# Output projection by quarters of the columns in a two-layer memory transformer with linear attention, with displaced rows through a DRAM scratch and a new order of work

## Chip, cores and metric

The kernel runs on one core of a Trainium2 chip. The metric is the device time of one execution in microseconds (us); the time of a kernel is the median over several runs. A profiled execution gives a trace of every instruction and every DMA packet of that one core.

## What is computed

The input is 2048 rows of 512 numbers. Four blocks follow each other, each adding to its input x: a recurrent-memory attention (A), a linear attention (B), A again and B again, with the same weights.

```python
# A, on h = layernorm(x); 64 segments of 32 rows, 32 heads of 128, 8 memory rows
mem = mem0
for s in range(64):
    h = concat([mem, xs[s]])                    # 40 x 512
    q, k, v = h @ Wq, h @ Wk, h @ Wv            # 40 x (32 heads x 128)
    p = softmax(mask(q @ k.T * 128 ** -0.5))    # per head, 40 x 40; memory rows see all
    o = (p @ v) @ Wo                            # 40 x 512
    mem = o[:8]; out[s] = o[8:]                 # mem feeds the next segment
x = x + out
# B, on layernorm(x): 32 heads of 16, phi(t) = where(t > 0, t + 1, exp(t)) + 1e-6
x = x + (phi(q) @ (phi(k).T @ v) / (phi(q) @ sum(phi(k)) + 1e-6)) @ wo
```

The memory rows make the 64 segments of a layer A one chain: segment s+1 can't project its memory rows before the output projection of segment s.

## The kernel before, in words

**Order of the work.** Every operation is recorded by `add` (L1632) as a node with a key such as (layer, step, 'out', 3). The table `PLACE` (L16 to L1555) gives each node a rank and, for copies that ScalarE (ACT) or VectorE (DVE) can both do, the engine. `schedule` (L1681) sorts all nodes by rank, gives PSUM banks, and `emit` (L1788) writes each engine's instructions in that order. So each engine runs a fixed list, in order, and waits on semaphores where a node needs another engine's result. Work that hangs on nothing late (the linear attention, the projections of rows that are known early) is put between the links of the chain by rank alone.

**Tiles on TensorE (PE).** Nearly all matmuls use a quarter of the array's columns: four matmuls with 32 columns of weights each, at tile positions (0, 0), (0, 32), (0, 64), (0, 96), write the four groups of 32 partitions of a PSUM bank. Such a four is the unit below. Each matmul stands in the program with a weight load of its own (LDWEIGHTS), except where the weights stay (`again`, L2075, seen in the trace as L2077).

**One segment step.** A block of 32 columns of hT holds 8 memory rows and 24 rows of the segment; the last 8 rows of each of four segments are collected in one more block, the left rows of the group (G counts groups of four segments, 128 rows). A step does:

- `kq0`, `kq1`, `v` (`project`, L2171, matmuls L2191 and L2077): keys, queries and values of the block, 512 columns a matmul; copies and 32x32 transposes turn them (L1954, L1955, L2210).
- `mem0`, `mem1` (`mem_attention`, L2295): scores (L2317, L2325), exp (L2332, L2336), values of the memory rows (L2353), division and transposes (L2358, L2360) into oTb.
- `out` (`out_proj`, L2431): the output projection of the memory rows of this segment and the other rows of the segment before it. Its operand is 32 rows by 4096 (32 heads by 128), and Wo_sb is 4096 by 512. The four of a tile position j splits as j = 2k + d: k picks one half of the contraction and d one half of the columns. So 16 fours of 256 columns (L2446) leave two partial sums for each half of the columns, one in partitions 0 to 63 and one in 64 to 127. A copy of the whole tile to outW_sb in float32 (128x256, L1954) is followed by a DVE addition of the two halves (64x256, L2458) into y_sb.
- `next` (`next_mem`, L2467): eight float32 matmuls (L2476) with outW_sb as weights and the selection matrix selm_sb as the moving operand add the two halves of the memory rows, transpose them, and a 32-column copy puts them into hT of the next segment.
- `x` (`x_attention`, L2373): the other rows' part of the attention (L2384, L2396, L2403, L2368, L2406, L2416, L2423, L2428).
- `res` (`residual`, L2495): `rows_out` (L2484) moves the 24 rows of y_sb straight to dx_sb in two DMAs, one issued by GpSimd (POOL) and one by SyncE (SP), both through `x_move` (L1970); in the last step of a group the left rows are projected by another `out_proj` and moved in eight small DMAs, and DVE adds dx_sb to x_sb (L2525). The layernorm of B and its sums (`b_in`, L2671) follow.

There are 162 output projections: 65 urgent ones and 16 of left rows in each of two layers. In the last group of a layer there is no move for the final rows; `pick` (L2506) adds them on PE from y_sb.

## Time and profile before

| what | value |
|---|---|
| median of 3 runs | 1513.69 us (1512.41 to 1515.43) |
| the profiled execution | 1513.92 us |
| its span, first to last instruction | 1512.0 us |
| granted TensorE clock | 0.998 |
| PE busy | 1458.4 us |
| DVE busy | 1227.5 us |
| ACT busy | 934.3 us |
| POOL busy | 199.5 us |
| DMA | 81639 packets, 60.26 MB |

How to read it: busy time of an engine is the union of its instructions' times. A matmul's recorded time includes its way through the array (a 128x256 one is recorded with 273 ns, though the fours follow each other faster), so a busy PE is not a PE at its peak; the pace is read from the starts of rows that follow each other in the timeline. PEld is the weight loading of PE, which runs beside the matmuls. "issue" as a releaser is idle time of an engine for which the profile shows nothing that it waited for. Queue q8 is the DMA queue that brings instructions. The kernel fills one core, so only that core's trace exists.

### The profile page before, as it was taken

How to read it: one execution, taken by the hardware profiler on the slowest of the kernel's cores; microseconds unless marked ns; L12 is line 12 of the kernel's file. 1: busy time of each engine (PE TensorE's matmuls, PEld its weight loads, DVE VectorE, ACT ScalarE, POOL GpSimd, SP SyncE). 2: the span in 40 equal slices, each digit the busy share in tenths (PEclk: the TensorE clock that was granted, in tenths of full speed). 3: DMA queues.
4: the chain of work that ended last, by engine and by line, in shares of the span. 5: the costliest groups of instructions: out<-in, count | busy, mean ns of one | idle time of the engine just before them, and what ended most of it. 6: DMA issues, size and time to landing. Idle time of an engine off the chain costs nothing.

```text
span 1512.0 us, 90803 instructions
## 1 busy us (share of the span) xinstructions
PE 1458.4 (96%) x43597; PEld 835.8 (55%) x39357; DVE 1227.5 (81%) x4035; ACT 934.3 (62%) x2686; POOL 199.5 (13%) x398
## 2 busy tenths in 40 slices
PE   7999999999999999999999999999999999999998
PEld 3455555555565555555545555555555555555554
DVE  4788888888888788788878888788887888887777
ACT  2566556665665656565566767666666755666656
POOL 3011110111111011111111110111111011111010
PEclk9999999999999999999999999999999999999999
DMA  9310100100000010001310101011110111011034
GB/s 390 106 35 21 35 14 23 25 24 24 25 21 11 23 25 24 25 23 32 64 25 21 28 18 27 25 28 28 25 22 20 26 24 28 20 28 32 16 49 134
DMA packets 81639, 60.26 MB, mean 40 GB/s; under 512 B 64040, under 2 KB 74600, under 8 KB 79720
## 3 DMA queue, kind: packets, MB, share of 16 engines
q1 hardware_dynamic: 67944, 37.58, 9.7%
q0 software_dynamic: 13152, 16.75, 4.0%
q8 instruction: 324, 5.31, 1.5%
q14 instruction: 59, 0.48, 0.1%
q10 hardware_dynamic: 160, 0.14, 0.0%
HBM read 25.57 MB, written 11.67 MB: 25 GB/s over the span
## 4 chain that ended last, share of the span: by engine, by line
PE 81%; DVE 8%; DMA 5%; ACT 3%; issue 1%; SPq 1%; POOL 0%; DVEq 0%
PE pb L2191 36%; PE pb L2446 18%; PE pb L2077 13%; PE pb L2089 3%; PE pb L2396 2%; PE pb L2633 2%; DMA dx_sb<-y_sb 2%; PE pb L2353 2%; PE pb L2416 2%; ACT arena_sb L1954 2%; PE pb L2317 1%; PE pb L2476 1%; DVE arena_sb L2210 1%; DVE arena_sb L1955 1%; DMA Wk_sb<-in_A_Wk_dram 1%
## 5 line engine op out<-in xcount | busy, mean ns | idle before, releaser
L1954 ACT ACTIVATE arena_sb<-pb 128x512 bf16<-128x512 f32 (+3 forms) x1021 | 512.0, 529 | 285.7 <-PE pb L2077 125.5
L2191 PE MATMUL pb<-Wk_sb,arena_sb 128*32 128x512 bf16 x4192 | 363.5, 382 | 5.5 <-DVE arena_sb L1955 2.5
L2191 PE MATMUL pb<-Wv_sb,arena_sb 128*32 128x512 bf16 x4608 | 340.1, 379 | 1.2 <-ACT arena_sb L1954 0.9
L2446 PE MATMUL pb<-Wo_sb,arena_sb 128*32 128x256 bf16 x10368 | 328.2, 273 | 5.7 <-issue 1.3
L2210 DVE STREAM_TRANSPOSE arena_sb<-arena_sb 128x256 f32<-128x256 f32 x640 | 259.9, 426 | 43.0 <-ACT arena_sb L1954 37.6
L2446 PEld LDWEIGHTS pb<-Wo_sb,arena_sb 128*32 128x32 bf16 x10368 | 261.5, 97 | 43.5 <-DVE arena_sb L2360 16.7
L2191 PE MATMUL pb<-Wq_sb,arena_sb 128*32 128x512 bf16 x3088 | 257.5, 379 | 1.3 <-DVE arena_sb L1955 1.1
L1971 POOL DMA_DIRECT2D dx_sb<-y_sb x246 | 125.0, 512 | 921.6 <-DVE y_sb L2458 401.3
L2191 PEld LDWEIGHTS pb<-Wk_sb,arena_sb 128*32 128x32 bf16 x4192 | 118.7, 97 | 184.9 <-issue 95.4
L2368 ACT ACTIVATE arena_sb<-pb,arena_sb 128x128 bf16<-128x128 f32 x536 | 166.8, 368 | 71.3 <-DVE arena_sb L2403 27.6
L2077 PE MATMUL pb<-Wq_sb,arena_sb 128*32 128x512 bf16 x2032 | 203.1, 381 | 0.0
L2191 PEld LDWEIGHTS pb<-Wv_sb,arena_sb 128*32 128x32 bf16 x4608 | 120.9, 96 | 94.5 <-issue 13.0
L2370 DVE TENSOR_TENSOR arena_sb<-pb,arena_sb 128x384 bf16<-128x384 f32 (+2 forms) x366 | 153.8, 421 | 7.9
L1955 DVE CAST arena_sb<-pb 128x512 bf16<-128x512 f32 (+2 forms) x239 | 117.8, 495 | 48.3 <-PE pb L2077 33.2
L1954 ACT ACTIVATE outW_sb<-pb 128x256 f32<-128x256 f32 (+1 forms) x156 | 59.7, 383 | 140.9 <-PE pb L2446 112.9
L2191 PEld LDWEIGHTS pb<-Wq_sb,arena_sb 128*32 128x32 bf16 x3088 | 86.1, 97 | 84.8 <-issue 24.2
L2384 DVE TENSOR_TENSOR arena_sb<-arena_sb,wx_sb 128x640 bf16<-128x640 bf16 x256 | 117.9, 472 | 2.9 <-ACT arena_sb L2336 2.1
L2396 PE MATMUL pb<-arena_sb 128*32 128x130 bf16 x3072 | 105.9, 220 | 1.4 <-issue 1.2
L2406 DVE STREAM_TRANSPOSE arena_sb<-arena_sb 128x192 f32<-128x192 f32 x256 | 93.2, 364 | 15.2 <-ACT arena_sb L2368 13.3
L2458 DVE TENSOR_TENSOR y_sb<-pb,outW_sb 64x256 bf16<-64x256 f32 x162 | 68.7, 424 | 38.2 <-ACT outW_sb L1954 34.4
L2077 PE MATMUL pb<-Wk_sb,arena_sb 128*32 128x512 bf16 x928 | 91.8, 379 | 0.1
L2396 PEld LDWEIGHTS pb<-arena_sb 128*32 128x32 bf16 x3072 | 68.4, 96 | 30.7 <-issue 7.8
(128 smaller groups left out, 1808.5 us busy)
## 6 DMA issues: line engine op xcount, KB each, us to landing
Wk_sb<-in_A_Wk_dram SPq DMA_DIRECT2D x1, 4096.0 KB, 14.9
Wq_sb<-in_A_Wq_dram SPq DMA_DIRECT2D x1, 4096.0 KB, 24.2
Wv_sb<-in_A_Wv_dram SPq DMA_DIRECT2D x1, 4096.0 KB, 33.6
Wo_sb<-in_A_Wo_dram SPq DMA_DIRECT2D x8, 512.0 KB, 23.2
xs_scratch<-x_sb POOLq DMA_DIRECT2D x32, 128.0 KB, 2.2
pq_scratch<-arena_sb POOLq DMA_DIRECT2D x27, 128.0 KB, 2.3
x_sb<-xs_scratch POOLq DMA_DIRECT2D x16, 128.0 KB, 3.4
dx_sb<-y_sb SPq DMA_DIRECT2D x126, 12.0 KB
```

The source lines that it names most:

```text
L1954: return e.activation(o() if callable(o) else o, i() if callable(i) else i, ACTF.Copy)
L1955: return e.tensor_copy(o() if callable(o) else o, i() if callable(i) else i)
L1971: add(eng, lambda e: e.dma_start(o, i), 0.55 if eng == "pool" else 0.66, reads=reads, writes=writes, dsem="%s%d" % (kind, k), lat=lat + (0 ...
L2077: return pe.add_instruction(mybir.InstMatmult(name=nc.get_next_instruction_name(), engine=mybir.EngineType.PE, ins=[pe.lower_ap(x), pe.low ...
L2191: r = pe.matmul(o, blk[:, c, :], w, start=(c == 0), stop=(c == 3), tile_position=(0, 32 * j))
L2210: add("dve", lambda v: v.transpose(dst, src(img[:, k, :].bitcast(F32))), 0.445, reads=[("img", k, h) for h in range(2)], writes=[dkey])
L2368: x = e.activation(o[:, u, :], i()[:, u, :], ACTF.Copy, scale=r[:, u:u + 1])
L2370: return e.tensor_tensor(o, i(), r.unsqueeze(2).to_broadcast([128, n, 128]), ALU.mult)
L2384: add("dve", lambda v, b=b: v.tensor_tensor(Px[:, b, :].rearrange("p (n j x) -> p n j x", n=20, j=4), PQ[:, r2, b, 64:224].rearrange("p (n ...
L2396: r = pe.matmul(pv.f32()[32 * i:32 * i + 32, 130 * k:130 * k + 130], cols(b, k, i), vimg[:, r2, 4 * b + i, :], start=True, stop=True, skip ...
L2406: add("dve", lambda v, b=b, k0=k0: v.transpose(oTb[:, s1, b, :, :, k0:k0 + 3].rearrange("p h j k q e -> p k (h j) (q e)").bitcast(F32), ox ...
L2446: r = pe.matmul(tl.f32()[32 * j:32 * j + 32, 0:256], oT[:, b, f, n, :, :, e], Wo_sb[:, 16 * b + 4 * n + 2 * f + e, 256 * d:256 * d + 256], ...
```

## The change

`out_proj` takes the four of a tile position as four quarters of the columns, each over the whole contraction: 32 fours of 128 columns instead of 16 of 256, and no partial sums. The result, 32 rows by 4 quarters in 128 partitions, goes into y_sb by one 128-column copy (ACT or DVE); outW_sb and the addition are gone. `next_mem` has four bfloat16 matmuls of 32 columns with y_sb as weights. y_sb has three buffers: two that take turns for the segments and one for left rows.

A row of y_sb now lies in four partitions, so displaced rows go through DRAM: each segment's 128x128 tile is written to `dy_scratch` by one POOL DMA (runs of 256 bytes), the left rows by four DMAs (two POOL, two SP), and one SP DMA per group reads 128 rows of 512 back into dx_sb; in the last group of a layer three DMAs do. `pick` has 16 matmuls of 128 columns instead of 8 of 256. The memset of half of y_sb is gone; two small tiles move within the arena.

All of `PLACE` is new: every rank, and in many places the choice between ACT and DVE.

```diff
-        def out_proj(oT, keys, urgent, end=False):
...
-                        for j in range(4):
-                            k, d = divmod(j, 2)
-                            n, f, e = 2 * k + (u + i) // 4, (u + i) // 2 % 2, (u + i) % 2
-                            r = pe.matmul(tl.f32()[32 * j:32 * j + 32, 0:256], oT[:, b, f, n, :, :, e],
-                                          Wo_sb[:, 16 * b + 4 * n + 2 * f + e, 256 * d:256 * d + 256], start=(hh == 0 and i == 0),
-                                          stop=(hh == 7 and i == 1), tile_position=(0, 32 * j))
+        def out_proj(oT, keys, k):
...
+                        for h in range(2):
+                            n, f, e = 2 * h + (u + i) // 4, (u + i) // 2 % 2, (u + i) % 2
+                            for j in range(4):
+                                r = pe.matmul(tl.f32()[32 * j:32 * j + 32, 0:128], oT[:, b, f, n, :, :, e],
+                                              Wo_sb[:, 16 * b + 4 * n + 2 * f + e, 128 * j:128 * j + 128],
+                                              start=(hh == 0 and i == 0 and h == 0), stop=(hh == 7 and i == 1 and h == 1),
+                                              tile_position=(0, 32 * j))
...
-            nd = evac(outW[cc, v, :], lambda: tl.f32()[cc, 0:256], 256, tiles=[tl], writes=[("outW", w)])
...
-            add("dve", lambda e: e.tensor_tensor(y, tl.f32()[a, 0:256], outW[c, v, :], ALU.add),
-                c_dve(256), reads=[("outW", w), "y0"], tiles=[tl], writes=[yk], quad=(2, 0) if urgent else (2, 1))
+            evac(y_sb[:, k, :], lambda: tl.f32()[:, 0:128], 128, tiles=[tl], writes=[("y", k)])
...
         def next_mem(s):
...
-            for h in range(2):
-                def mm(pe, h=h):
-                    for j in range(4):
-                        o = 128 * h + 32 * j
-                        r = pe.matmul(tl.f32()[32 * j:32 * j + 32, 16 * h:16 * h + 16], outW[:, w, o:o + 32],
-                                      selm_sb[:, :], start=True, stop=True, tile_position=(0, 32 * j))
+            def mm(pe):
+                for j in range(4):
+                    r = pe.matmul(tl.f32()[32 * j:32 * j + 32, 0:32], y_sb[:, k, 32 * j:32 * j + 32], selm_sb[:, :],
+                                  start=True, stop=True, tile_position=(0, 32 * j))
...
-        def rows_out(k, G, moves):
...
-                    x_move(dx_sb[dst:dst + n, G % 2, 256 * d:256 * d + 256], y_sb[32 * d + src:32 * d + src + n, k, :], k,
-                           [("y", k)], [("dx", G % 2, dst, d)], ("dy", "dz")[d], ("pool", "sp")[d])
+        def dy_view(G):
+            return dy_dram[layer * NT + G].rearrange("(g r) (q x) -> q g r x", g=4, q=4)
...
+            for q in range(4):
+                x_move(dy_view(G)[q, :, 32:40, :], y_sb[32 * q:32 * q + 32, k, :], q, [("y", k)], [("dyl", layer, G, q)], "dz",
+                       ("pool", "sp")[q % 2])
...
+            x_move(dy_view(G)[:, g, 0:32, :], y_sb[:, w, :], w, [("y", w)], [("dy", layer, G, g)], "dy")
...
+                    x_move(dx_sb[:, G % 2, :], dy_dram[layer * NT + G].rearrange("(g r) x -> g r x", g=4)[:, 8:40, :], G % 2,
+                           [("dy", layer, G, i) for i in range(4)] + [("dyl", layer, G, q) for q in range(4)], [("dx", G % 2)], "ddx", "sp")
```

## The prediction

> **What bounds the kernel now.** I read the page first: busy time by engine, then the shares of the chain that ended last.

> ```profile
> span 1512.0 us, 90803 instructions
> PE 1458.4 (96%) x43597; PEld 835.8 (55%) x39357; DVE 1227.5 (81%) x4035; ACT 934.3 (62%) x2686; POOL 199.5 (13%) x398
> PE 81%; DVE 8%; DMA 5%; ACT 3%; issue 1%; SPq 1%; POOL 0%; DVEq 0%
> q8 instruction: 324, 5.31, 1.5%
> ```

> PE is the limit: it idles 53.6 us (1512.0 - 1458.4), and 81% of the chain is PE's own work. What PE's time is made of is read from the starts of rows in the timeline of PE; columns are start, duration, line, form, count.

> ```profile
> 701.89 1.93 PE L2446 MATMUL pb<-Wo_sb,arena_sb 128*32 128x256 bf16 x64
> 703.64 0.82 PE L2633 MATMUL pb<-arena_sb 128*32 128x512 bf16 x12
> 704.30 0.32 PE L2476 MATMUL pb<-selm_sb,outW_sb 128*32 128x16 f32 x16
> 704.45 0.24 PE L2396 MATMUL pb<-arena_sb 128*32 128x130 bf16 x4
> ...
> 705.00 0.40 PE L2191 MATMUL pb<-Wk_sb,arena_sb 128*32 128x512 bf16 x4
> 705.22 0.40 PE L2077 MATMUL pb<-Wq_sb,arena_sb 128*32 128x512 bf16 x4
> ...
> 711.11 0.27 PE L2704 MATMUL pb<-arena_sb 128*32 128x32 bf16 x16
> 711.21 0.29 PE L2416 MATMUL pb<-arena_sb 128*32 128x130 bf16 x8
> ...
> 1483.77 0.62 PE L2089 MATMUL pb<-arena_sb 128*32 128x128 bf16 x32
> 1484.21 0.60 PE L2633 MATMUL pb<-arena_sb 128*32 128x512 bf16 x8
> ```

> From start to next start: a projection's 64 matmuls take 1.75 us (109 ns a four); the float32 group of `next` 0.15 us; a four of 512 columns 0.22 us; a four of 32 columns 25 ns; a four of 128 columns 55 ns (0.44 us for 8).

> The second limit is easy to miss. Queue q8 brought 324 packets. PE and PEld together ran 43597 + 39357 = 82954 instructions, and 82954 / 324 = 256: each packet is a page of 256 PE instructions. How fast can pages come? The waits of PE put down to "issue" (line, total us, times, longest), one of them in the timeline, and the windows around it (bounds, length, then busy us and instructions of PE and PEld) answer:

> ```profile
> PE pb L2476 <- issue: 4.5, 3, 1.6
> PE pb L2446 <- issue: 1.3, 4, 0.4
> PE pb L2396 <- issue: 1.2, 3, 0.7
> PE pb L2416 <- issue: 0.6, 1, 0.6
> ```

> ```profile
> 627.55 0.24 PE L2476 MATMUL pb<-selm_sb,outW_sb 128*32 128x16 f32 x2
> 629.42 0.28 PE L2476 MATMUL pb<-selm_sb,outW_sb 128*32 128x16 f32 x11 [1.63 <-issue]
> ```

> ```profile
> 618.60:626.90 8.30, 7.34 (x211) 5.02 (x199) 6.78 (x24) 6.23 (x20) 1.64 (x3) 1.00 0.25 68
> 627.00:629.40 2.40, 0.79 (x46) 0.59 (x35) 0.99 (x3) 0.95 (x3) 0.52 (x1) 1.00 0.04 10
> 629.40:630.60 1.20, 1.18 (x35) 0.69 (x30) 0.78 (x6) 0.05 (x1) 0.00 (x0) 1.00 0.14 34
> 1163.41:1165.97 2.56, 2.56 (x132) 2.23 (x132) 2.41 (x12) 1.87 (x7) 0.00 (x0) 1.00 0.26 51
> ```

> The DMA view of these windows has no q8 row for 618.6 to 626.9 and none for 629.4 to 630.5, and one packet each here (627.0 to 629.5, then 629.4 to 630.6):

> ```profile
> q8 instruction: 1, 0.02, 2.2%
> ```

> ```profile
> q8 instruction: 1, 0.02, 5.8%
> ```

> So for 8.3 us no page arrived, PE ran some 410 instructions and then stood still inside `next` until 2.4 us after the late packet began; the next page was asked for 1.1 us after that. With no page in reserve a page costs **2.4 + 1.1 = 3.5 us**, or 73 instructions per us. PE's mean demand is 82954 / 1512 = 55 per us, so today this shows only as 7.6 us of issue waits. The last window shows how much a dense stretch may run ahead: 264 instructions in 2.56 us without a wait, 0.94 us less than 3.5.

> **The change part by part.**

> *Matmuls of the projection.* 16 fours of 256 columns become 32 of 128: 32 x 55 ns = 1.76 us against 1.75. With 57 ns a four (a little over the row) it is +0.07. I take +0.03 us, times 162 projections: **+5 us** (0 to +11).

> *`next`.* 0.15 us becomes one four of 32 columns, 0.025: -0.12 us x 126 = **-15 us**, all on PE (the count is in the row below, 2016 / 16). `pick` keeps its pace (16 x 128 columns for 8 x 256). Setup copies: nothing, they stand beside the weights' loading.

> ```profile
> L2476 PE MATMUL pb<-selm_sb,outW_sb 128*32 128x16 f32 x2016 | 40.2, 186 | 6.4 <-issue 4.5 <-ACT outW_sb L1954 1.2 <-DVE outW_sb L1955 0.2
> L2458 DVE TENSOR_TENSOR y_sb<-pb,outW_sb 64x256 bf16<-64x256 f32 x162 | 68.7, 424 | 38.2 <-ACT outW_sb L1954 34.4
> L1954 ACT ACTIVATE outW_sb<-pb 128x256 f32<-128x256 f32 x124 | 47.6, 384 | 129.7 <-PE pb L2446 102.8 <-PE pb L2396 24.9 <-PE pb L2711 1.4
> ```

> *Copies.* DVE loses 162 additions, 68.7 us; the copies, 0.384 us now, halve their columns. Neither engine is the limit, so this is worth only PE's waits on them: at most the 46 us of idle time left without issue. The addition stands behind the chain, the copy in it; the new order has both engines carrying other copies in the room gained. I take **-20 us** (-46 to +20, since an entirely new order can also place a link too tightly).

> *Displaced rows.* Per segment one POOL DMA replaces one of POOL and one of SP; per group four replace eight, and an SP load is added that waits for all of them. Queued behind that load on SP are the transposes of layernorm, behind the addition on DVE everything of the chain.

> ```profile
> xs_scratch<-x_sb POOLq DMA_DIRECT2D x32, 128.0 KB, 2.2
> x_sb<-xs_scratch POOLq DMA_DIRECT2D x16, 128.0 KB, 3.4
> L2525 DVE TENSOR_TENSOR x_sb<-x_sb,dx_sb 128x512 bf16<-128x512 bf16 x30 | 12.2, 406 | 5.8 <-DMA dx_sb<-y_sb 4.9 <-issue 0.8
> ```

> Nearest rows: a write to DRAM lands in 2.2 us, a load in 3.4. The built order of the changed kernel has about 3.3 us of PE work between write and load and 3.7 between load and addition in most groups, so both legs are covered: **0 us** (-5, today's waits there gone, to +30, one us late in each of 30 groups).

> *Instructions.* This is the largest term. 162 projections get 64 more matmuls and 64 more loads each (+20736), `next` sheds 3024: 100666, or 393 pages. A projection is now 256 instructions in 1.76 us: a full page in half of what a page costs. With the 192 instructions of a segment's attention (scores, values: 14 fours at 56 ns, 10 at 25 to 30) a step has a dense run of some 448 instructions in 2.8 us, 160 per us against 73, and after it projections of 512 columns with some 25 to 37 per us, during which only one page can be fetched ahead. A page wholly inside the dense run leaves PE dry for 3.5 - 1.76 = 1.7 us, less what it had in hand (0.94 by the last window): 0.8 to 1.7 us, in most of 128 steps.

> For the sum I cut the order of the changed program (it holds no times) into pages of 256 and gave each page its PE time by the paces above. Of 393 pages 212 last under 3.5 us, short by 223 us together: the upper end, nothing in hand. Against 2.56 us 133 pages are short by 55 us: the lower end, the full 0.94 in hand at every page. The same ledger of the kernel before gives 41 and 0.5 us, and 7.9 us against 3.0, where the trace shows 7.6. Against 2.8 and 3.0 the changed order gives 91 and 124 us. I take their middle, 108, less the 8 paid already: **+100 us** (+50 to +215).

> [...]

> *Sum*, against the profiled execution's own span: 1512 + 5 - 15 - 20 + 0 + 100 = 1582. Outside the span lie 1.9 us (1513.92 - 1512.0): **1584 us**. That execution stands 0.2 us above the median of 1513.69, which changes nothing here.

> **The rivals.**

> 1. *Pages keep up* (the faster side). If pages are asked for further ahead than the stall suggests, or twice at a time, only the PE work and the waits remain: 1512 + 5 - 15 - 15 + 2 = 1489. For it: only 11 issue waits among 324 pages, and the window of 264 instructions in 2.56 us. Against it: the measured 2.4 + 1.1 us. It decides from a page cost of about 1.9 us downwards, where a projection's page no longer waits. Chance 0.13.

> 2. *The weight load sets the pace.* One of 97 ns for each four instead of 55 would make a projection 32 x 0.101 = 3.2 us:

> ```profile
> L2446 PEld LDWEIGHTS pb<-Wo_sb,arena_sb 128*32 128x32 bf16 x10368 | 261.5, 97 | 43.5 <-DVE arena_sb L2360 16.7
> ```

> 261.5 us over 2592 fours are 101 ns a four, which fits loads one after another as well as four beside each other. Price (3.23 - 1.75) x 162 = +240: 1512 - 15 + 240 - 10 + 2 = 1729. Against it: the 32 matmuls at 1483.77, each with its own load, took 0.44 us. Chance 0.02. [...]

> 3. *The detour is late.* Both DRAM legs one us over the placed distance in 30 groups, with DVE held in order: 60 us on top of rival 1, 1549. The 2.2 and 3.4 us rows speak against it. Chance 0.02.

> 4. *Nothing moves*: PE's savings are eaten by new waits, 1511 to 1517. PE's share of 96% speaks against exact balance. Chance 0.04.

> **How the numbers follow.** Forecast 0.79, at 1584. Its range: the page term from 55 (less 8) with all waits gone, 1512 - 10 - 46 + 47 + 2 = 1505, up to 150 with no wait gained, 1512 - 10 + 150 + 2 = 1654; the 215 needs nothing ever in hand, which the 2.56 us window excludes. I give 1500 to 1655, which leaves rivals 1 and 2 and the tails outside. A difference of 0.2% is about what a measurement of this kernel can tell from no change. Slower by more: forecast and rivals 2 and 3, 0.83. Within: 0.03. Faster: rival 1 and the edge of rival 4, 0.14.

> **What would show it.** q8 near 393 packets. PE waits put down to issue near 100 us instead of 7.6, of 0.5 to 1.7 us, inside or right after the projection's matmuls, about one per segment, with a q8 packet begun some 2.4 us before each end. Where PE is not dry, a projection of 128 matmuls in 1.75 to 1.8 us. the addition into x_sb waiting under 10 us for its load. DVE near 1170 us busy. Wrong if: issue waits stay under 20 us (rival 1), the projection runs evenly at 100 ns a four (rival 2), or DVE waits for dx_sb by 50 us (rival 3).

## The result, and the profile after

The changed kernel takes **1662.82 us** (median of four runs, 1658.15 to 1667.08), the kernel before beside it 1514.56 (1512.41 to 1515.71): a ratio of 1.098 (95% interval 1.0944 to 1.1016), 148 us more. The forecast was 1584 in a range of 1500 to 1655: the direction and the mechanism hold, the size does not.

The page of the changed kernel: span, busy time by engine, the chain that ended last by engine, and the queue that brings instructions.

```profile
span 1656.3 us, 108079 instructions
PE 1486.8 (90%) x52469; PEld 872.7 (53%) x48229; DVE 1198.1 (72%) x3943; ACT 874.2 (53%) x2518; POOL 201.7 (12%) x338
PE 86%; issue 8%; DVE 3%; DMA 1%; ACT 1%; SPq 0%
q8 instruction: 394, 6.46, 1.6%
```

PE idles 169.5 us where it idled 53.6. "issue" has 8% of the chain for 1%, DVE 3% for 8% and DMA 1% for 5%. The queue brought 394 pages of 256 PE instructions for 324. The waits of PE in the same run (line, what ended the wait, total us, times, longest us):

```profile
PE pb L2433 <- issue: 72.1, 80, 2.0
PE pb L2387 <- issue: 20.7, 19, 1.8
PE pb L2182 <- issue: 12.9, 17, 2.4
PE pb L2407 <- issue: 9.3, 8, 2.0
PE pb L2455 <- issue: 5.1, 5, 1.9
PE pb L2455 <- ACT y_sb L1953: 3.9, 15, 0.4
```

L2433 is the projection, L2387 and L2407 the values of the segment's attention, L2455 `next`. All issue waits together, with four smaller lines, are 128.3 us for 7.6. How one of them looks is read in the timeline of PE (start, duration, line, form, count, idle time before it):

```profile
705.56 0.62 PE L2433 MATMUL pb<-Wo_sb,arena_sb 128*32 128x128 bf16 x32
706.01 0.20 PE L2316 MATMUL pb<-arena_sb 128*32 128x64 bf16 x4
...
706.14 0.84 PE L2433 MATMUL pb<-Wo_sb,arena_sb 128*32 128x128 bf16 x48
706.81 0.21 PE L2316 MATMUL pb<-arena_sb 128*32 128x64 bf16 x4
...
708.48 0.35 PE L2433 MATMUL pb<-Wo_sb,arena_sb 128*32 128x128 bf16 x11
709.64 0.27 PE L2433 MATMUL pb<-Wo_sb,arena_sb 128*32 128x128 bf16 x5 [0.82 <-issue]
...
710.91 1.45 PE L2433 MATMUL pb<-Wo_sb,arena_sb 128*32 128x128 bf16 x87
713.39 0.55 PE L2433 MATMUL pb<-Wo_sb,arena_sb 128*32 128x128 bf16 x25 [1.03 <-issue]
```

Where PE is not dry, 32 matmuls take 0.45 us and 48 take 0.67: 56 ns a four, so the projection itself is not slow. But it stops inside a four that has begun, after 11 and after 87 matmuls, where no semaphore stands. From 709.64 to 713.39, a page apart, are 3.75 us. The DMA views of 707.0 to 709.6 and of 710.6 to 713.3 show one packet of queue q8 each; the row of the first view is:

```profile
q8 instruction: 1, 0.02, 2.7%
```

By the trace's packet starts these begin at 707.29 and 710.79, so PE resumes 2.4 and 2.6 us after its packet begins.

The two parts of the change that could have been late are in the groups by line: the addition of the displaced rows into x (count, busy us, mean ns, idle time before it) and the copy of the projection on ACT.

```profile
L2516 DVE TENSOR_TENSOR x_sb<-x_sb,dx_sb 128x512 bf16<-128x512 bf16 (+1 forms) x32 | 12.9, 403 | 0.3 <-DMA dx_sb<-dy_scratch 0.3
L1953 ACT ACTIVATE y_sb<-pb 128x128 bf16<-128x128 f32 x137 | 37.9, 277 | 198.5 <-PE pb L2433 155.3 <-PE pb L2387 41.1 <-PE pb L2701 1.7
```

The detour through DRAM costs 0.3 us of waiting in the whole run.

To give the page term one number I cut each run's PE and PEld instructions, in the order of their starts, at every 256th, and added up by how much the matmul at each cut starts later than the pace of its shape would have it. The kernel before has 19.6 us at its cuts, the changed one 162.8: **+143 us** of the 144.3 by which the spans differ. At all other places the late starts are 71.9 and 70.2 us.

The waits themselves show where the cuts are. Counting in the instructions of PE's sequencer that the trace also holds (some 164, nearly all of them waits on semaphores), all 141 issue waits of the changed kernel and all 11 of the kernel before come 193 or 194 instructions beyond a multiple of 256: each stands at the edge of a page.

How much is put down to the cuts depends a little on the count. A second one takes the pace of each shape from the medians of the same two traces and counts lateness wherever PE falls behind that pace. It gives 17 and 169 us at the cuts (+152), 88 and 86 elsewhere (-2) and 5 us less work at full pace, together the 144.

### The profile page after: what moved, and what is told of

Read it like the earlier page. It is cut to its first block, busy times and chain, and to the rows that moved or that the text cites. A ratio compares the mean times of both kernels' runs of the same rounds, so it can differ in the third digit from the quotient of the medians.

```text
span 1656.3 us, 108079 instructions
## 1 busy us (share of the span) xinstructions
PE 1486.8 (90%) x52469; PEld 872.7 (53%) x48229; DVE 1198.1 (72%) x3943; ACT 874.2 (53%) x2518; POOL 201.7 (12%) x338
## 4 chain that ended last, share of the span: by engine, by line
PE 86%; issue 8%; DVE 3%; DMA 1%; ACT 1%; SPq 0%
PE pb L2182 39%; PE pb L2433 19%; PE pb L2070 14%; PE pb L2387 3%; PE pb L2082 3%; PE pb L2623 2%; PE pb L2344 2%; PE pb L2407 2%; PE pb L2308 2%; DMA Wk_sb<-in_A_Wk_dram 1%; PE pb L2455 1%; DVE arena_sb L1954 1%; PE pb L2316 1%; ACT arena_sb L1953 0%; ACT y_sb L1953 0%
## 5 line engine op out<-in xcount | busy, mean ns | idle before, releaser
L2433 PE MATMUL pb<-Wo_sb,arena_sb 128*32 128x128 bf16 x20736 | 369.8, 220 | 74.3 <-issue 72.1
L2182 PE MATMUL pb<-Wk_sb,arena_sb 128*32 128x512 bf16 x4192 | 376.6, 385 | 16.9 <-issue 7.1
L2433 PEld LDWEIGHTS pb<-Wo_sb,arena_sb 128*32 128x32 bf16 x20736 | 321.0, 97 | 133.6 <-issue 90.3
L2182 PE MATMUL pb<-Wq_sb,arena_sb 128*32 128x512 bf16 x3088 | 266.6, 380 | 4.6 <-issue 2.7
L1954 DVE CAST arena_sb<-pb 128x512 bf16<-128x512 f32 (+2 forms) x277 | 134.1, 487 | 156.2 <-PE pb L2387 50.6
L1971 POOL DMA_DIRECT2D dy_scratch<-y_sb x186 | 124.8, 672 | 1002.6 <-ACT y_sb L1953 528.8
L2070 PE MATMUL pb<-Wq_sb,arena_sb 128*32 128x512 bf16 x2032 | 211.5, 385 | 1.6 <-issue 1.6
L2361 DVE TENSOR_TENSOR arena_sb<-pb,arena_sb 128x384 bf16<-128x384 f32 (+2 forms) x402 | 176.7, 441 | 9.6
L2359 ACT ACTIVATE arena_sb<-pb,arena_sb 128x128 bf16<-128x128 f32 x403 | 128.2, 368 | 94.7 <-DVE arena_sb L2414 35.8
L1953 ACT ACTIVATE y_sb<-pb 128x128 bf16<-128x128 f32 x137 | 37.9, 277 | 198.5 <-PE pb L2433 155.3
L2387 PE MATMUL pb<-arena_sb 128*32 128x130 bf16 x3072 | 118.7, 221 | 20.7 <-issue 20.7
L2387 PEld LDWEIGHTS pb<-arena_sb 128*32 128x32 bf16 x3072 | 71.9, 96 | 49.3 <-issue 33.3
L2070 PE MATMUL pb<-Wk_sb,arena_sb 128*32 128x512 bf16 x928 | 93.0, 379 | 0.6 <-issue 0.6
L2407 PE MATMUL pb<-arena_sb 128*32 128x130 bf16 x2048 | 71.1, 221 | 10.5 <-issue 9.3
## 6 DMA issues: line engine op xcount, KB each, us to landing
xs_scratch<-x_sb POOLq DMA_DIRECT2D x32, 128.0 KB, 2.5
dx_sb<-dy_scratch SPq DMA_DIRECT2D x30, 128.0 KB
pq_scratch<-arena_sb POOLq DMA_DIRECT2D x27, 128.0 KB, 2.3
```

The costliest lines, as they stand in the source:

```text
L1953: return e.activation(o() if callable(o) else o, i() if callable(i) else i, ACTF.Copy)
L1954: return e.tensor_copy(o() if callable(o) else o, i() if callable(i) else i)
L1971: add(eng, lambda e: e.dma_start(o, i), 0.55 if eng == "pool" else 0.66, reads=reads, writes=writes, dsem="%s%d" % (kind, k), lat=lat + (0 ...
L2070: return pe.add_instruction(mybir.InstMatmult(name=nc.get_next_instruction_name(), engine=mybir.EngineType.PE, ins=[pe.lower_ap(x), pe.low ...
L2182: r = pe.matmul(o, blk[:, c, :], w, start=(c == 0), stop=(c == 3), tile_position=(0, 32 * j))
L2359: x = e.activation(o[:, u, :], i()[:, u, :], ACTF.Copy, scale=r[:, u:u + 1])
```

## The experiments

My theory: the changed kernel is slower because a dense run of PE instructions uses pages up faster than one page at a time can be fetched. Its rivals: each four's weight load sets the pace, the detour or the new order is late, or pages keep up. All times below are medians beside runs of the kernel before on the same chip; runs 4 and 5, which measure PE alone, are single executions.

**1. The kernel before, with twice the projection's instructions.** Order, detour and sum of halves stay as they were.

```diff
-    for j in range(4):
-        ... tl[.., 0:256] <- Wo_sb[.., 256 * d:256 * d + 256]
+    for c in range(2):
+        for j in range(4):
+            ... tl[.., 128 * c:128 * c + 128] <- Wo_sb[.., 256 * d + 128 * c:256 * d + 128 * c + 128]
```

> The kernel before, with one edit: each 256-column matmul of the output projection becomes two of 128 columns, each with its own weight load (256 instructions a projection instead of 128). Order of work, sum of halves, copies, DMAs all stay. Theory (pages of 256 PE instructions cost some 3.5 us each): 103,853 instructions, 405 pages; short by 270 us against 3.5 us a page, where the changed kernel's were short by 223 and lost 143 more than before, so some 150 to 175 us are added: 1665 to 1690 us. Rival 'the new order of work is to blame': 1515 to 1525. Rival 'the DRAM detour or its DMAs are to blame': 1515 to 1525. Rival 'weight loads set the pace of narrow matmuls': slower too, with even 100 ns fours and few issue waits.

1721.35 us beside 1509.98, ratio 1.1406 (1.1363 to 1.1448): +211 us, 31 us above the range that I expected. The page and the largest wait of PE:

```profile
q8 instruction: 405, 6.64, 1.6%
```

```profile
PE pb L2448 <- issue: 96.6, 90, 2.5
```

With no detour, no new order and the same columns computed, instructions alone cost more than the whole change. 217 us are late at the page cuts, 198 more than before.

**2. The same split, but the second half of each pair keeps the weights.** As many loads as before, 10368 more matmuls.

```diff
+    if c:
+        r = again(pe, y, oT[..], x, s, t, (0, 32 * j), True)
```

> The kernel before with each 256-column matmul of the output projection split into two of 128 columns, the second four reusing the weights that are loaded (192 instructions a projection: 128 matmuls, 64 loads). Pages theory: 93,485 instructions, 365 pages, short by 139 us against 3.5 us a page (before: 41), so some 50 to 75 us are added: 1565 to 1590 us. Rival 'weight loads set the pace': no more loads than before, so 1515 to 1525. Rivals order and detour: 1515 to 1525.

1588.34 us, ratio 1.0513 (1.0483 to 1.0543): +78 us, 365 pages, 93 us late at the cuts. This is the upper edge of what the pages theory gave, and no weight load was added. The projection now stands on two lines: the first half of each pair on L2453, the second on L2077, together with other matmuls that keep their weights. The largest waits of PE, and the projection's own group on L2077 (count, busy us, mean ns, idle time before it):

```profile
PE pb L2453 <- issue: 15.4, 20, 1.6
PE pb L2077 <- issue: 11.6, 18, 1.2
PE pb L2396 <- issue: 11.3, 14, 1.6
```

```profile
L2077 PE MATMUL pb<-Wo_sb,arena_sb 128*32 128x128 bf16 x10368 | 328.3, 219 | 11.4 <-issue 11.0
```

So the projection has 15.4 + 11.0 = 26.4 of the 65.4 us of issue waits in this run, 40%; it has 72.1 of 128.3 in the changed kernel and 96.6 of 178.5 in run 1, more than half. The rest falls on the work beside it: the stall goes to whoever stands at the page's end.

**3. The changed kernel with the wide matmuls of before.** The order, the copies and the detour stay changed.

```diff
-    for h in range(2):
-        for j in range(4):
-            ... tl[.., 0:128] <- Wo_sb[.., 128 * j:128 * j + 128]
+    for j in range(4):
+        ... tl[.., 0:256] <- Wo_sb[.., 256 * d:256 * d + 256]
```

> The changed kernel with its new order, copies, next and DRAM detour, but the projection's matmuls are those of before: 16 fours of 256 columns (128 instructions). Left out: the two halves of the contraction are not added, and only 128 of the 256 columns are copied on. Pages theory: 80,124 instructions, 312 pages, short by 20 us against 3.5 us (before: 41), so nearly all of the loss goes: 1490 to 1510 us. Rivals 'new order' and 'DRAM detour': 1640 to 1665, as the changed kernel. Weight loads: 1490 to 1510 too.

1489.26 us, ratio 0.9871 (0.9848 to 0.9895). The page and the projection's issue waits:

```profile
PE 1440.2 (97%) x42101; PEld 799.7 (54%) x37861; DVE 1194.7 (81%) x3943; ACT 874.0 (59%) x2518; POOL 201.5 (14%) x338
q8 instruction: 313, 5.13, 1.4%
```

```profile
PE pb L2433 <- issue: 0.9, 2, 0.7
```

With 81 pages fewer the late starts at the cuts are 7.9 us, and everything else of the change is no longer slow. The order and the detour are not the cause. But this run leaves out the sum of the halves, and that turned out to matter (runs 7 to 10).

**4. What a page costs, PE alone.** Bursts of fours, one kind after another, with slow stretches (kept weights, 512 columns) between them; the last burst beside loads of 4 MB from DRAM.

```diff
+    sparse(pe)
+    fours(pe, 512, 128, True)
+    sparse(pe)
+    fours(pe, 512, 128, False)
+    sparse(pe)
+    fours(pe, 256, 256, True)
+    sparse(pe)
+    fours(pe, 1024, 32, True)
+    sparse(pe).then_inc(s_pe, 1)
+    fours(pe, 512, 128, True)
```

> A measurement of the page cost by itself. Nothing of the reference is computed: the output is zeros, and PE runs five dense stretches on a matrix of ones, with a stretch of 90 fours of 512 columns without loads before each, so that pages can be brought ahead. Stretches: 512 fours of 128 columns with loads (4096 instructions, 16 pages); the same without loads (2048, 8 pages); 256 fours of 256 columns with loads (2048, 8 pages); 1024 fours of 32 columns with loads (8192, 32 pages); the first again beside 4 MB loads from DRAM. Pages theory: 16 x 3.5 = 56 us, about 28, about 28, 32 x 3.5 = 112, and the last longer than the first if other DMAs slow the page; PE runs at full pace for at most 512 instructions before it first stands still. [...]

The kernel took 401.53 us. In the timeline of PE the count is one of matmuls; where each has a load, 128 of them are a page:

```profile
24.18 2.51 PE L32 MATMUL pb<-one_sb 128*32 128x128 bf16 x167
27.98 1.97 PE L32 MATMUL pb<-one_sb 128*32 128x128 bf16 x128 [1.30 <-issue]
31.44 1.97 PE L32 MATMUL pb<-one_sb 128*32 128x128 bf16 x128 [1.49 <-issue]
...
79.08 1.66 PE L32 MATMUL pb<-one_sb 128*32 128x128 bf16 x93 [1.76 <-issue]
...
148.19 28.36 PE L32 MATMUL pb<-one_sb 128*32 128x256 bf16 x1028
...
200.06 1.19 PE L32 MATMUL pb<-one_sb 128*32 128x32 bf16 x128 [2.00 <-issue]
...
307.73 0.62 PE L32 MATMUL pb<-one_sb 128*32 128x32 bf16 x5 [2.52 <-issue]
...
335.03 3.56 PE L32 MATMUL pb<-one_sb 128*32 128x128 bf16 x128 [2.98 <-issue]
...
368.74 3.18 PE L32 MATMUL pb<-one_sb 128*32 128x128 bf16 x128 [2.88 <-issue]
```

The dense burst runs 167 matmuls and their loads at full pace, 334 instructions, then exactly one page between stalls: (79.08 - 27.98) / 14 = **3.65 us a page**. By the count of 256 the burst began some 80 instructions before the end of a page, so the 334 are that rest and one whole page more. With 32 columns, where a page holds a quarter of the columns, it is (307.73 - 200.06) / 30 = 3.59, at a clock granted at only 0.51: the price belongs to the instructions, neither to the width of the matmul nor to the clock. At 256 columns with loads (1028 matmuls without a break; the next row starts at 176.36) a page lasts 3.5 us and nothing stalls. Beside the loads from DRAM six pages take 33.7 us, 5.6 each. By the trace's packet starts 3.1 to 4.2 us pass there between PE's restart and the next packet after four of five restarts, where 1.1 do after the loads. The clock was granted at 0.74 there, and a page's 128 matmuls are recorded with up to 3.61 us for 1.97, but that is not the whole reason: one of these pages ran at full clock, PE ran out of instructions at 347.25, and the next packet began 1.6 us after that; in the first burst it begins 0.8 to 0.9 us before PE runs out.

These rows also settle the weight loads: the first 167 matmuls carry one each and run at 55 ns a four.

**5. How much is in hand when a dense run begins.** PE alone again, in cycles of 784 instructions, so that the page cut moves by 16 each time; the dense run has 256, 448 and 640 of them.

```diff
+    for dense, slow in ((32, 66), (56, 42), (80, 18)):
+        for i in range(16):
+            fours(pe, dense, 128, True)
+            r = fours(pe, slow, 512, True)
```

> No part of the kernel's computation: PE alone runs 16 cycles each of a dense run (fours of 128 columns, each matmul with its load) and a slow run (fours of 512 columns with loads): 256 + 528, 448 + 336 and 640 + 144 instructions, 784 a cycle, so that the page boundary moves by 16 instructions each cycle. It asks what PE has in hand when a dense run of the changed kernel's length begins. [...]

The waits and parts of the timeline (676.46 us in all):

```profile
PE pb L31 <- issue: 52.3, 46, 2.0
```

```profile
24.25 259.54 PE L31 MATMUL pb<-one_sb 128*32 128x128 bf16 x6439
284.79 12.26 PE L31 MATMUL pb<-one_sb 128*32 128x128 bf16 x384 [1.00 <-issue]
...
482.97 12.26 PE L31 MATMUL pb<-one_sb 128*32 128x128 bf16 x384 [1.05 <-issue]
496.55 1.97 PE L31 MATMUL pb<-one_sb 128*32 128x128 bf16 x128 [1.32 <-issue]
500.30 6.64 PE L31 MATMUL pb<-one_sb 128*32 128x128 bf16 x256 [1.77 <-issue]
...
669.90 4.32 PE L31 MATMUL pb<-one_sb 128*32 128x128 bf16 x89 [1.50 <-issue]
```

The 16 cycles with 256 dense instructions run without a stall (6272 of the first row's 6439 matmuls; the other 167 begin the next kind). With 448 there is one stall a cycle, in 14 of 16 cycles, 13.2 us from 284.79 to 482.97. With 640 the other 32 waits add 39.1 us. Each stall also costs about 0.2 us that counts as busy (128 matmuls at 55 ns a four are 1.76, the rows above say 1.97). So a cycle loses (13.2 + 14 x 0.2) / 16 = 1.0 us and (39.1 + 32 x 0.2) / 16 = 2.8 us. Against them stands an estimate for the same time in hand at every page: the instructions of a cycle cut into pages, 55 ns a dense four and 0.22 us a slow one, each page counted as far as it is short of a threshold. With 2.56 us (0.94 in hand) a cycle of 448 loses 0.7 us and one of 640 1.3, with the 2.9 that I took 1.1 and 2.0, with 3.5 to 3.6 (nothing in hand) 1.9 to 2.0 and 3.2 to 3.4. The measured 1.0 lies between the first two, the 2.8 between the last two. No one number fits both. What fits both: **something is in hand once for each dense run, not at every page**. Cut at the pages, page and stall last 3.1 us here after a page that did not stall, and 3.6 after one that did.

**6. The kernel before, with the copied halves in bfloat16**, the part of the change that takes the float32 passes out of `next`.

```diff
-    selm_sb = sb("selm_sb", [128, 16], F32)
+    selm_sb = sb("selm_sb", [128, 16])
-    outW = sb("outW_sb", [128, NW - 1, 256], F32)
+    outW = sb("outW_sb", [128, NW - 1, 256])
```

> The kernel before, its order untouched, with one thing changed: the copied half sums and the 16-column selection matrix are bfloat16 instead of float32, so that `next` is 8 bfloat16 matmuls in place of 16 float32 passes (each half sum is rounded to bfloat16 before the halves are added). Pages: 324 become about 316. If the float32 form of `next` is all that PE's own work can gain from the new projection (step `next`), PE loses 0.10 us x 126 = 13 us and the time falls to 1495 to 1502. If that time only turns into waits on the copies ahead of it, it stays within 3 us of the kernel before.

1505.29 us beside 1510.91, ratio 0.9965 (0.995 to 0.9981). That is 5.6 us less, between the two expectations, and the only kernel here that computes all and beats both. PE's busy time falls by 10.4 us, from 1458.4, so the work saved reaches the time only in part:

```profile
PE 1448.0 (97%) x42589; PEld 810.7 (54%) x38349; DVE 1226.1 (82%) x4035; ACT 933.7 (62%) x2686; POOL 199.7 (13%) x398
```

**7 to 10. The changed order with wide matmuls, and the halves really added.** Run 3 left the sum out. Run 7 sends both halves through the scratch and adds both into x; run 8 brings each half back by one load instead of two; run 9 adds the halves on DVE right behind the copy, so that the scratch carries no more than in the changed kernel; run 10 places that addition up to four places later.

Run 7, against run 3:

```diff
+    evac(y_sb[:, k, :], lambda: tl.f32()[:, 0:256], 256, ..)
+    dy_dram = [2 * NT, 4, 160, 256]
+    for h in range(2):
+        add("dve", .. x[0:n, :] + dx_sb[0:n, 2 if h else G % 2, :])
```

> The changed kernel's order of work, bfloat16 copies and route through DRAM scratch, but with the 256-column projection of before (halves of the contraction, 64 matmuls): the halves are copied once in bfloat16, each goes to the scratch by itself, and both are loaded and added into x (two additions a group), `next` has 8 matmuls. Pages about 316. Pages theory: everything that cost the changed kernel its time is gone, and what it won stays: 1488 to 1500, issue waits of PE under 10 us. Rival (the sum of the halves, which the run with wide matmuls in the changed order left out, is what the change bought its gain with): 1508 or more, with PE or DVE waiting for the second addition or its loads.

Run 8, against run 7:

```diff
-    dy_dram = [2 * NT, 4, 160, 256]
+    dy_dram = [2 * NT, 160, 4, 256]
```

> The kernel of the run with both halves sent through the scratch, with one thing changed: the scratch keeps the four quarters of a row side by side, so that each group's two halves come back by one load each (two DMAs on SP's queue in place of four, same bytes). In the run before it the additions into x waited 43.9 us for these loads (39 waits, 1.1 us each), and four loads took SP 2.21 us to issue, 0.55 each. If the detour was late by SP's issuing, the last load starts 1.1 us earlier and most of that wait goes: under 15 us of waits on dx_sb and 1495 to 1525. If the order itself is worse with halves, or the doubled bytes are what is late, the wait stays at 30 us or more and the time at 1540 or more.

Run 9, against run 3:

```diff
+    evac(yp_sb[:, k, :], lambda: tl.f32()[:, 0:256], 256, ..)
+    add("dve", .. y_sb[0:64, k, :] = tl.f32()[64:128, 0:256] + yp_sb[0:64, k, :])
```

> The changed kernel's order and its route through DRAM scratch, with the 256-column projection of before, whole: the halves are copied in bfloat16, `next` takes the halves (8 matmuls), and one addition on DVE right behind the copy makes the 32 summed rows, so that the scratch carries the same bytes as in the changed kernel (one 32 KB write a segment, one 128 KB load a group). If the two runs with halves in the scratch were slow because their doubled bytes landed late, this one is only about 0.55 us later at each write than the run with wide matmuls: the additions into x wait under 15 us for the load, and the time is 1490 to 1510. If having two halves to add costs what the order won whatever way it is done (DVE then waits for the copies and PE for DVE), 1530 or more.

Run 10, against run 9 (t is the addition's rank, w[0][0] that of the write):

```diff
+    t = max(t, min(t + 4, w[0][0] - 1))
```

> As the run with the sum on the chip, but with the addition of the halves placed up to four places later in the order, still ahead of the write that takes its result, so that DVE need not stand and wait for ACT's copy. If DVE's wait at that addition is what the sum costs, this is 3 to 15 us faster than the other; if the write's lateness is, the two agree within 3 us or this one is slower.

They took 1558.95 (ratio 1.0327, 1.0295 to 1.0358), 1545.29 (1.0197, 1.0181 to 1.0213), 1562.42 (1.0321, 1.03 to 1.0342) and 1553.88 us (1.0261, 1.0239 to 1.0283). None has more than 317 pages or 17 us late at the cuts. My first expectations for 7 and 9 were wrong, by 59 and 52 us from their upper ends; the rival named with each, that the sum of the halves costs what the order won, came true. The waits, of DVE and of PE in run 7, of DVE in run 8, and of DVE in runs 9 and 10:

```profile
DVE x_sb L2541 <- DMA dx_sb<-dy_scratch: 43.9, 39, 1.8
...
PE pb L2443 <- DVE arena_sb L2361: 31.1, 18, 3.2
```

```profile
DVE x_sb L2540 <- DMA dx_sb<-dy_scratch: 32.6, 37, 1.5
```

```profile
DVE y_sb L2453 <- ACT yp_sb L1957: 41.2, 85, 1.3
...
DVE x_sb L2535 <- DMA dx_sb<-dy_scratch: 8.3, 13, 1.3
```

```profile
DVE y_sb L2456 <- ACT yp_sb L1960: 30.9, 56, 1.3
```

With doubled bytes the addition into x waits for the scratch, 1.1 us each time, and DVE, which works through its fixed list, passes that on to PE's next link of the chain (L2361 is a transpose of the attention): ahead of 15 of these 18 waits of PE, 30.2 of the 31.1 us, such an addition had waited and begun 0.6 to 1.4 us before PE went on. Half the loads take 11.3 us of that wait away and, by the ratios, 1.3% of the time, 20 us, of which up to 6 go with the clock (0.990 in run 7, 0.994 in run 8). That is the second of the outcomes named for run 8: the wait stays above 30 us and the time above 1540. With the bytes of the changed kernel the scratch is nearly in time (8.3 us), but DVE now waits for ACT's copy instead; moved later, that wait loses 10.3 us and the time 8.5, as expected if DVE's wait is a part of what the sum costs. In none of these four ways did the changed order have room for a second operation behind the copy; an order made for the halves was not tried. How the rest of the 56 to 73 us between these runs and run 3 divides among DVE's extra work, ACT's longer copy and the chain was not tried apart.

## Why the prediction was right and where it failed

- **What bounds the kernel** was right: PE, and behind it the supply of its instructions. 394 pages (393 predicted); the stalls stand in and right after the projection, and nineteen of twenty end 2.2 to 2.9 us after their packet's start. Issue waits are 128.3 us where about 100 were named, and DVE is busy for 1198 us instead of 1170.
- **The page term** was right in kind and mis-sized: +100 predicted, **+143** measured (+152 by the second count). The step that failed is the ledger's threshold, "their middle" between 2.8 and 3.0, that is a page of 3.5 us with 0.5 to 0.7 us in hand at every page. In the changed kernel, cut at its pages, those that carry under 3.0 us of PE work and stall last 3.4 us with their stall after a page that did not stall (97 of them) and 3.8 after one that did (38). So the page is dearer than the one stall that I had read (3.6 with PE alone; that the DMA traffic of the kernel makes the rest is argued from run 4's last burst, not shown), and what is in hand is spent by the first stall. The same ledger, done again with the pages of the two traces, gives 157 us for the changed kernel and 17 for the one before against 3.2 us a page, and 177 and 23 against 3.3: the measured difference lies there and not at 2.9. The window of 264 instructions in 2.56 us that I took for the reserve at every page was the first page of a run; the page ahead of it had lasted 5.6 us.
- **Waits on DVE and ACT, -20**: -2 by the late starts away from the cuts. Run 3, which has hardly any page stalls, has 68.3 us of them for 71.9: without stalls the change frees 4 us, not 20. I had taken idle time without "issue" to be mostly the copies' doing, where the new order keeps it. A term that the sum did not have hides in the -2: the clock. It was granted at 0.990 in the changed kernel (0.989 to 0.991 in its four runs) and at 0.998 before, at most 0.010 x 1656 - 0.002 x 1512 = 14 us. After the first 30 us the trace has 27 us at half the clock (3 us in the kernel before), and in them PE starts 15 us late away from the cuts (2 us). Without that the waits would have fallen by some 15 us. Why the clock is lower is open: run 7 has 0.990 without page stalls, run 2 has 0.997 with them.
- **PE work, +5 and -15**: the projection's four runs at 56 ns, so 32 x 56 = 1.79 us, +0.04 x 162 = +7; `next` goes down by 0.11 (its four starts 0.04 us ahead of the next row), -14. That makes -7 for -10. The late starts of the first count leave +3 where this says -7; the second count leaves -5 and puts the difference at the cuts.
- **The detour, 0**: right, 0.3 us of waits.
- **The range** failed at its top, which stood for 150 us at the cuts, no wait gained, and 10 us less work of PE: 1654. The first two came nearly so, and of the 10 us at most 7 did; the profiled execution took 1658.15 us and the median lies 5 us above it.
- **Rival 1** (pages keep up, 1489) is near what run 3 takes with 313 pages, 1489.26, and is refuted for 394 by runs 1 and 4. That the two agree within 1 us is chance: run 3 gains 12 us at the cuts and 4 in waits, where the rival had 15 in waits. **Rival 2** (loads set the pace) is refuted by the rows at 56 ns, by run 4, and by run 2, which is slower with no load added. **Rival 3** (the detour late by one us in each group, 1549) did not happen in the changed kernel; run 7 meets its condition, 1.1 us late, and takes 1559, run 8 1545. **Rival 4** is refuted by the result.

That the sum of the halves is gone and that pages run short are two sides of one trade: the whole contraction in each column group is what makes 32 fours of 16, and without it the same order paid for the second operation on DVE in all four ways tried.

## What to carry to other kernels

Count instructions, not only columns: divide the instructions of PE and its weight loads by the page size that the instruction queue shows, and compare the time of each dense stretch with the price of a page read from a stall (3.65 us in run 4's first burst). A reserve read in one window belongs to the start of a dense run, where page and stall lasted 3.1 us in run 5 and 3.4 in the changed kernel; charge every further page of that run its whole price, 3.6 and 3.8 there. And before leaving a reduction to the matmul, ask what the other engine's list has room for: an order made for one copy may not take a copy and an addition.
